# Spreading the reciprocal denominators of linear attention over 128 features: one-hot matmuls into PSUM, or a DMA inside SBUF that repeats each row 16 times

## The chip, the cores and the metric

The kernel runs on one core of one Trainium2 chip. The metric is the device time of one execution in microseconds (us), as the median of several runs. Engines are named as in the profile: PE is the matmul engine and PEld its weight load, DVE the vector engine, ACT the scalar engine, POOL the general one, SP the engine whose queue issues the DMAs. Each engine works through its own list of instructions in order and waits on semaphores for the others.

## The reference: what is computed

The input x has 2048 tokens of 512 features. Four layers follow each other, attention A, dense B, A, B, each added to its input. An A layer has 32 heads of 16 features:

```
q, k, v = split_heads(layernorm(x) @ wqkv)
pq, pk  = phi(q), phi(k)                    # phi(t) = t+1 for t > 0, else exp(t); + 1e-6
kv  = sum over tokens of pk^T v             # 16 x 16 a head
z   = sum over tokens of pk                 # 16 a head
o   = (pq @ kv) / (pq . z + 1e-6)           # one denominator for each token and head
x   = x + merge_heads(o) @ wo
```

A B layer is `x + relu(layernorm(x) @ w1) @ w2` with 1376 hidden features.

The change concerns the division. A denominator belongs to a head, and it has to reach the 16 features of that head.

## The kernel before, in words

**Tiling.** Tokens go in four chunks t of 512. The feature-by-token tiles of phi(q) stand in the SBUF tensor `big`, one unit of 128 features x 512 tokens (bf16) for each chunk t and feature group j = 0..3, so a unit holds 8 heads. All matmuls but the transposes and the warm-up are issued by one helper, `mm_group`, so they all show as line 507 and are told apart by their tiles.

**An A layer** runs in this order (`layer_steps`, L739 to L817). `p1(t)`: k projections and phi (L490, L492, L494, L500), and the sums z. `pq(t)`: q projections of chunks 0 to 2. `bar` (L763): the last sums z and the masked table `Zc` (L541); the denominators `a_den(t)` of chunks 0 to 2; the products `a_g` of xn with phi(k) for four row blocks m; `a_g_evac` (GT, L556 or L557); `a_kv`; `a_m`, which masks kv into `KVT` (L566) and multiplies it with wo into `Mf` (L573 or L574); then the q projections and the denominator of chunk 3. `p2(t)` (L784): `a_fin` for four token tiles, which multiplies phi(q) with `Mf` and adds the residual (L518); layernorm for the next layer (L436 to L461), and its transposition into `Tb`, for chunk 0 on PE (L478), for the others by a DMA on SP (L464).

**The denominators.** `a_den(t)` multiplies phi(q) with `Zc`, which puts the eight heads of group j on rows 32j to 32j+7 of one PSUM bank. ACT takes the logarithm (`lnd`, L592) and the exponential of its negative (`rdc`, L594), so `rdc` holds reciprocals in bf16. `a_pqs(t)` (L597) then multiplies each reciprocal into the 16 features of its head: four matmuls with the one-hot table `Esel` (32 rows x 128 columns each) spread the rows into four PSUM banks, and DVE multiplies `big` by each of them (L603). `Esel` is made once at the start by `head_rows` (L417), with one transposition (L419) and one DVE copy (L421).

**What sets the order.** The program is a graph of operations, each with an engine, the keys that it reads and writes, and an assumed cost in ns. `_list_schedule` (L117) walks it once on the host: of the operations that are ready within a window of each engine's list it takes the one that starts first, and so fixes for each engine a static order. It also gives out the eight PSUM banks. `a_pqs` takes four banks at once. A DMA is an operation of the SP queue with an assumed 60 ns of issue; its data are assumed to land 1.4 us after the issue at the earliest, plus the transfer time that its caller gives, one after the other over all DMAs, plus 0.6 us (L225 to L229). The multiply L603 is planned at 600 ns, ACT passes from PSUM at 495 ns. At run time each instruction of an engine waits for its semaphores, and everything behind it on that engine waits too.

Of the kernel before, what the change touches and what calls it, by code (L numbers as in the profile page):

```python
# [7 lines left out]
ALU = alu_op_type.AluOpType  # L8
ACTF = mybir.ActivationFunctionType
BF16 = mybir.dt.bfloat16  # L10
F32 = mybir.dt.float32

PE, ACT, DVE, POOL, SP = "pe", "act", "dve", "pool", "sp"
# [3 lines left out]
C_MM128 = 58.0  # L17
# [8 lines left out]
C_DVE_PSUM = 600.0  # L26
# [217 lines left out]
def build_kernel(nc, A_x, A_wqkv, A_wo, B_w1, B_w2, out, n_layers_pairs=2, K_STT=0, Q_STT=0, A_PE_CHUNKS=1, windows=None,  # L244
# [10 lines left out]
    NCH = NT // 4  # L255
# [9 lines left out]
    with es:  # L265
        def sb(name, shape, dt):
            return es.enter_context(nc.sbuf_tensor(name, list(shape), dt))
# [10 lines left out]
        KVT = sb("KVT", [128, 4, 128], BF16)  # L278
        Mf = sb("Mf", [128, 4, 512], BF16)
        NL = 2  # L280
        lnd = sb("lnd", [128, NL, 512], F32)
        rdc = sb("rdc", [128, NCH, 512], BF16)
        hm128 = sb("hm128", [128, 4, 32], BF16)
        hm1 = sb("hm1", [128, 4, 32], F32)
        Esel = sb("Esel", [128, 128], BF16)
        Zc = sb("Zc", [128, 4, 32], BF16)
        ones1 = sb("ones1", [128, 2], BF16)
        lnw = sb("lnw", [128, 2], F32)
        big = sb("big", [128, UNITS * 512], BF16)
# [21 lines left out]
        ident = sb("ident", [128, 128], BF16)  # L311
        bmask = sb("bmask", [128, 128], BF16)
        ps = es.enter_context(nc.psum_tensor("ps", [128, 8, 512], F32))
# [4 lines left out]
        g = _Graph()  # L318
# [4 lines left out]
        def alloc_bank():  # L323
            return g.new_tile()
# [7 lines left out]
        psv = _PS()  # L332
# [3 lines left out]
        def dma(emit, reads, writes, xfer_ns, name):  # L336
            sem = es.enter_context(nc.semaphore("dsem%d" % len(dma_sems)))
            dma_sems.append(sem)

            def _emit(eng, emit=emit, sem=sem):  # L340
                return emit(eng).then_inc(sem, 16)
            op = g.add(SP, _emit, reads, writes, dur=C_SP_ISSUE, lat=xfer_ns, dma=True, name=name)
            op.seq = sem
            return op
# [14 lines left out]
        def unit_ap(u, p=128):  # L359
            return big[0:p, u * 512:(u + 1) * 512]  # L360
# [30 lines left out]
        if WARM > 0:  # L391
            wt = alloc_bank()

            def _warm(e):
# [18 lines left out]
              [("onesf",)], [("hm1",)], 350, name="as_h1")  # L413
        g.add(POOL, lambda e: e.affine_select(hm128[:], hm1[:], [[0, 4], [16, 32]], ALU.is_ge, 0.0, base=15, channel_multiplier=-1),
              [("hm1",)], [("hm128",)], 350, name="as_h2")

        def head_rows():  # L417
            b = alloc_bank()
            g.add(PE, lambda e: e.transpose(psv[:, b, 0:64].bitcast(BF16), hm128[:].rearrange("p j r -> p (j r)"), ident[:]),  # L419
                  [("hm128",), ("ident",)], [("ps", b)], C_MM128, name="trh")  # L420
            g.add(DVE, lambda e: e.tensor_copy(Esel[:], psv[:, b, 0:64].bitcast(BF16)), [("ps", b)], [("Esel",)], 200.0, name="esel")  # L421

        def ln_stats_first(i):
            g.add(DVE, lambda e: e.bn_stats(bst[:, i, :], xin[:, i, :]), [("xin", i)], [("bst", i)], C_DVE_BNST, name="bnst%d" % i)  # L424
# [78 lines left out]
        def mm_group(mk, reads, writes, dur, name):  # L503
            def _emit(e, mk=mk):
                last = None
                for (o, l, r, st, sp, skip) in mk():
                    last = e.matmul(o, l, r, start=st, stop=sp, skip_group_check=skip)  # L507
                return last
            return g.add(PE, _emit, reads, writes, dur, name=name)
# [45 lines left out]
        def a_g_evac(m, GB):  # L555
            g.add_flex([(ACT, lambda e: e.activation(GT[:, m, :], psv[:, GB, :], ACTF.Identity), C_ACT_PSUM),  # L556
                        (DVE, lambda e: e.tensor_copy(GT[:, m, :], psv[:, GB, :]), C_DVE_FLEX)],  # L557
                       [("ps", GB)], [("GT", m)], name="gev%d" % m)
# [27 lines left out]
        def a_den(t):  # L586
            b = alloc_bank()
            s = scr_state["ln"]
            scr_state["ln"] = (s + 1) % NL
            mm_group(lambda: [(psv[32 * j:32 * j + 32, b, :], Zc[:, j, :], unit_ap(pq_unit(j, t)), True, True, False) for j in range(4)],  # L590
                     [("Zc",)] + [("big", pq_unit(j, t)) for j in range(4)], [("ps", b)], 400.0, "den%d" % t)
            g.add(ACT, lambda e: e.activation(lnd[:, s, :], psv[:, b, :], ACTF.Ln, bias=1e-6, scale=1.0),  # L592
                  [("ps", b)], [("lnd", s)], C_ACT_PSUM, name="lnd%d" % t)
            g.add(ACT, lambda e: e.activation(rdc[:, t, :], lnd[:, s, :], ACTF.Exp, scale=-1.0),  # L594
                  [("lnd", s)], [("rdc", t)], C_ACT_EXP, name="rdc%d" % t)

        def a_pqs(t):  # L597
            bs = [alloc_bank() for _ in range(4)]
            mm_group(lambda: [(psv[:, bs[j], :], Esel[32 * j:32 * j + 32, :], rdc[32 * j:32 * j + 32, t, :], True, True, False) for j in range(4)],
                     [("Esel",), ("rdc", t)], [("ps", b) for b in bs], 400.0, "rdx%d" % t)  # L600
            for j in range(4):
                u = pq_unit(j, t)
                g.add(DVE, lambda e, j=j, u=u: e.tensor_tensor(unit_ap(u), unit_ap(u), psv[:, bs[j], :], ALU.mult),  # L603
                      [("ps", bs[j]), ("big", u)], [("big", u)], C_DVE_PSUM, name="pqs%d_%d" % (t, j))

        def a_fin(i, first_layer):
            t, il = i // 4, i % 4
# [117 lines left out]
            tr_state["first"] = False  # L725
            transpose_chunk(t, extra_reads=extra)
        ln_first(0)
        head_rows()

        def ln_next(t, on_pe=False):  # L730
            ln_chunk(t, False)
# [7 lines left out]
        def layer_steps(layer):  # L739
            first_layer = layer == 0  # L740
            last_layer = layer == NLAYERS - 1
            steps = []
            if layer % 2 == 0:
                ZB = alloc_bank()
                KB = alloc_bank()
                GB = [alloc_bank() for _ in range(4)]

                def p1(t):
                    if first_layer and t + 1 < NCH:
                        ln_first(t + 1)  # L750
                    for i in range(4 * t, 4 * t + 4):
                        a_k(i)
                    if t >= 1:
                        for i in range(4 * t - 4, 4 * t):
                            a_z(i, ZB)
                    if first_layer and t >= 1:
                        for m in range(2):
                            a_g(m, 4 * t - 4, GB[m])

                def pq(t):  # L760
                    a_q(t)

                def bar():  # L763
                    for i in range(NT - 4, NT):
                        a_z(i, ZB)
                    a_zc(ZB)
                    for t in range(NCH - 1):
                        a_den(t)
                    n = 0
                    for m in range(4):  # L770
                        for s in range(NCH - 1 if (first_layer and m < 2) else 0, NCH):
                            a_g(m, 4 * s, GB[m])
                            n += 1
                            if n in (3, 5, 7):
                                a_pqs((n - 3) // 2)
                        a_g_evac(m, GB[m])
                        if m >= 1:
                            a_kv(m - 1, KB)
                    a_kv(3, KB)
                    a_m(KB)  # L780
                    a_q(NCH - 1)
                    a_den(NCH - 1)

                def p2(t):  # L784
                    for i in range(4 * t, 4 * t + 4):
                        a_fin(i, first_layer)
                    ln_next(t, t < A_PE_CHUNKS)
                    if t == 0:
                        a_pqs(NCH - 1)

                if first_layer:
                    for t in range(NCH):
                        steps.append((t, None, lambda t=t: p1(t)))
                        if t < NCH - 1:
                            steps.append((None, None, lambda t=t: pq(t)))
                else:
                    for t in range(NCH):
                        steps.append((t, None, lambda t=t: p1(t)))
                    for t in range(NCH - 1):
                        steps.append((None, None, lambda t=t: pq(t)))  # L800
                steps.append((None, None, bar))
                for t in range(NCH):
                    steps.append((None, t, lambda t=t: p2(t)))
            else:
                def o_step(t):
                    for i in range(4 * t, 4 * t + 4):
                        b_out(i, last_layer)
                    if last_layer:
                        store_chunk(t)
                    else:  # L810
                        ln_next(t)
                for t in range(NCH):
                    steps.append((t, None, lambda t=t: b_h(t)))
                    if t >= 1:
                        steps.append((None, None if last_layer else t - 1, lambda t=t: o_step(t - 1)))
                steps.append((None, None if last_layer else NCH - 1, lambda: o_step(NCH - 1)))
            return steps  # L817
# [129 lines left out]
```

## Time and profile before

| What | Value |
|---|---|
| Median of three runs | 295.43 us (295.38 to 295.44) |
| Profiled execution | 295.29 us, of which the span of the instructions is 293.6 us |
| PE busy | 286.7 us, 98% |
| ACT busy | 172.3 us, 59% |
| DVE busy | 156.8 us, 53% |
| POOL busy | 33.0 us, 11% |
| Granted PE clock, all 40 slices | nine tenths or more |
| DMA traffic | 15.66 MB; queue q1 busy 21.5% of 16 engines |

The table is read from the top: the profiled execution is 0.14 us under the median, and 1.69 us of it lie outside the span. A busy PE is not PE at its peak, since matmuls are pipelined: a 128x512 matmul shows as some 380 ns, while in a row of sixteen the starts are 0.216 us apart. Lines are given with a start in us from the beginning of the span, a duration, engine, line, operation, the tiles out<-in, and in square brackets the idle time of that engine before it with what ended it. The first A layer reaches its `bar` at about 46 us and the next layer at about 72 us; the second A layer does so at about 178 and 212 us.

### The profile page before, as it was taken

To read this page: it belongs to the slowest core of one execution; us is meant where nothing else is said; L and a number is where in the kernel's file an instruction comes from. 1 tells how busy PE (TensorE), PEld (TensorE's weight loads), DVE (VectorE), ACT (ScalarE), POOL (GpSimd) and SP (SyncE) were. 2 spreads that over 40 slices of the span, in tenths; PEclk is the share of its full clock that TensorE was granted. 3 is DMA by queue.
4 is the path that set the end of the run, shared out by engine and by line. 5 is a ranking of instruction groups with operands and counts; after the bars stand their busy time and mean duration, and the time that the engine had idled before them with its cause. 6 is when DMAs were issued, how large, how long until landed. Compare 5 with 4: busy or idle time off the path is not lost.

```text
span 293.6 us, 4046 instructions
## 1 busy us (share of the span) xinstructions
PE 286.7 (98%) x1540; PEld 132.0 (45%) x1540; DVE 156.8 (53%) x441; ACT 172.3 (59%) x352; POOL 33.0 (11%) x43
## 2 busy tenths in 40 slices
PE   7899999999999999999999999999999999999996
PEld 3354444334444444444444443444444444444444
DVE  5899674999700481351453758938971036020123
ACT  2997596687865484388334899258786406307000
POOL 3102100002500050020020300000260002000000
PEclk9999999999999999999999999999999999999999
DMA  7993310000330034030006300000033002301022
GB/s 224 356 370 73 65 18 0 2 0 1 74 71 0 0 65 80 1 71 2 0 0 74 73 0 2 0 0 2 1 71 74 0 0 73 73 5 66 0 74 71
DMA packets 33443, 15.66 MB, mean 53 GB/s; under 512 B 25264, under 2 KB 32912, under 8 KB 33424
## 3 DMA queue, kind: packets, MB, share of 16 engines
q1 hardware_dynamic: 33424, 15.40, 21.5%
q8 instruction: 12, 0.20, 0.3%
q14 instruction: 7, 0.06, 0.1%
HBM read 7.01 MB, written 2.10 MB: 31 GB/s over the span
## 4 chain that ended last, share of the span: by engine, by line
PE 88%; DVE 6%; DMA 2%; ACT 2%; SPq 1%; issue 0%
PE ps L507 88%; DMA xin<-in_A_x_dram 2%; DVE big L603 2%; DVE xn L456 1%; DVE xres L518 1%; ACT Mf L573 1%; ACT big L490 1%; PE ps L478 0%; DVE bst L424 0%; DVE big L500 0%; DVE emscr L494 0%; ACT sqscr L524 0%; SPq L371 0%; ACT escr L492 0%; SPq L370 0%
## 5 line engine op out<-in xcount | busy, mean ns | idle before, releaser
L507 PE MATMUL ps<-w,big 128*128 128x512 bf16 (+2 forms) x363 | 77.3, 372 | 0.0
L507 PE MATMUL ps<-Tb,w 128*128 128x512 bf16 (+1 forms) x352 | 77.1, 379 | 0.0
L628 ACT ACTIVATE big<-ps 128x512 bf16<-128x512 f32 (+1 forms) x73 | 43.2, 599 | 27.9 <-PE ps L507 27.7
L524 ACT ACTIVATE sqscr<-xres 128x512 bf16<-128x512 f32 x48 | 30.0, 629 | 41.5 <-DVE xres L518 40.6
L507 PEld LDWEIGHTS ps<-Tb,w 128*128 128x128 bf16 (+1 forms) x352 | 35.2, 100 | 40.9
L507 PEld LDWEIGHTS ps<-w,big 128*128 128x128 bf16 (+1 forms) x363 | 35.2, 97 | 40.3
L490 ACT ACTIVATE big<-ps 128x512 bf16<-128x512 f32 x64 | 41.0, 644 | 8.0 <-PE ps L507 7.8
L518 DVE SCALAR_TENSOR_TENSOR xres<-ps,xres 128x512 f32<-128x512 f32 x32 | 21.9, 687 | 41.3 <-PE ps L507 41.1
L492 ACT ACTIVATE escr<-ps 128x512 bf16<-128x512 f32 x64 | 41.3, 662 | 0.4 <-DVE emscr L494 0.4
L444 POOL TENSOR_TENSOR rstd<-veps,nhalf 128x4 f32<-128x4 f32 x15 | 16.1, 1072 | 203.8 <-DVE veps L442 183.6
L515 DVE TENSOR_TENSOR xin<-ps,xres 128x512 bf16<-128x512 f32 x15 | 10.4, 692 | 48.3 <-PE ps L507 48.3
L507 PE MATMUL ps<-wqkv,Tb 128*128 128x512 bf16 x128 | 29.6, 379 | 1.4 <-ACT Tb L482 1.1
L507 PE MATMUL ps<-Tb,wqkv 128*128 128x512 bf16 x128 | 30.6, 379 | 0.0
L507 PE MATMUL ps<-Mf,big 128*128 128x512 bf16 x128 | 29.5, 379 | 1.0 <-ACT Mf L573 0.8
L507 PE MATMUL ps<-big,xn 128*128 128x512 bf16 x128 | 30.3, 379 | 0.0
L494 DVE TENSOR_SCALAR emscr<-escr 128x512 bf16<-128x512 bf16 x64 | 18.3, 294 | 18.7 <-ACT escr L492 18.6
L500 DVE TENSOR_TENSOR big<-big,emscr 128x512 bf16<-128x512 bf16 x64 | 26.3, 420 | 1.2
L603 DVE TENSOR_TENSOR big<-big,ps 128x512 bf16<-128x512 bf16 x32 | 19.8, 678 | 1.3 <-PE ps L507 1.3
L507 PEld LDWEIGHTS ps<-wqkv,Tb 128*128 128x128 bf16 x128 | 12.1, 98 | 16.2 <-ACT Tb L482 1.5
L507 PEld LDWEIGHTS ps<-Mf,big 128*128 128x128 bf16 x128 | 11.9, 98 | 16.2 <-ACT Mf L573 1.3
L507 PEld LDWEIGHTS ps<-big,xn 128*128 128x128 bf16 x128 | 11.5, 97 | 13.1 <-issue 1.5
L507 PEld LDWEIGHTS ps<-Tb,wqkv 128*128 128x128 bf16 x128 | 11.5, 97 | 12.3 <-DVE big L603 0.4
(69 smaller groups left out, 181.2 us busy)
## 6 DMA issues: line engine op xcount, KB each, us to landing
wqkv<-in_A_wqkv_dram SPq DMA_DIRECT2D x3, 512.0 KB, 6.1
xin<-in_A_x_dram SPq DMA_DIRECT2D x3, 512.0 KB, 7.9
out_dram<-xin SPq DMA_DIRECT2D x3, 512.0 KB, 2.9
w<-in_B_w_dram SPq DMA_DIRECT2D x1, 1376.0 KB, 10.9
w<-in_B_w_dram SPq DMA_DIRECT2D x1, 1280.0 KB, 12.9
wo<-in_A_wo_dram SPq DMA_DIRECT2D x1, 512.0 KB, 8.9
xin<-in_A_x_dram SPq DMA_DIRECT2D x1, 384.0 KB, 3.0
out_dram<-xin SPq DMA_DIRECT2D x1, 256.0 KB, 2.1
```

Of the source, the lines that this page charges most:

```text
L444: g.add(POOL, lambda e: e.tensor_tensor(rstd[:, sl], veps[:, sl], nhalf[:, 0:4], ALU.pow), [("veps", t), ("nhalf",)], [("rstd", t)], C_POO ...
L456: (DVE, lambda e: e.tensor_scalar(xn[:, i, :], src, rstd[:, i:i + 1], nbias[:, i:i + 1], ALU.mult, ALU.add), C_DVE_NORM_BF if first else 4 ...
L490: g.add(ACT, lambda e: e.activation(dst_ap, psv[:, b, :], ACTF.Identity, bias=1.0 + 1e-6, scale=1.0), [("ps", b)], [dst_key], C_ACT_PSUM, ...
L492: g.add(ACT, lambda e: e.activation(escr[:, s, :], psv[:, b, :], ACTF.Exp), [("ps", b)], [("escr", s)], C_ACT_EXP, name=name + "_exp")
L494: g.add(DVE, lambda e: e.tensor_scalar(emscr[:, s, :], escr[:, s, :], 1.0, 1e-6, ALU.min, ALU.add), [("escr", s)], [("emscr", s)], C_DVE_B ...
L500: g.add(DVE, lambda e: e.tensor_tensor(dst_ap, dst_ap, emscr[:, s, :], ALU.max), [dst_key, ("emscr", s)], [dst_key], 340.0, name=name + "_ ...
L507: last = e.matmul(o, l, r, start=st, stop=sp, skip_group_check=skip)
L515: g.add(DVE, lambda e: e.tensor_tensor(xin[:, i, :], psv[:, b, :], src, ALU.add), [("ps", b), skey], [("xin", i)], C_DVE_PSUM, name="resid ...
L518: g.add(DVE, lambda e: e.scalar_tensor_tensor(xres[:, i, :], psv[:, b, :], 0.0, src, ALU.add, ALU.add, accum_out=s1[:, i:i + 1]), [("ps", ...
L524: g.add(ACT, lambda e: e.activation(sqscr[:, q, :], xres[:, i, :], ACTF.Square, accum_out=s2[:, i:i + 1]), [("xres", i)], [("sqscr", q), ( ...
L603: g.add(DVE, lambda e, j=j, u=u: e.tensor_tensor(unit_ap(u), unit_ap(u), psv[:, bs[j], :], ALU.mult), [("ps", bs[j]), ("big", u)], [("big" ...
L628: g.add_flex([(ACT, lambda e, M=M, b=b, u=u: e.activation(unit_ap(u, M), psv[0:M, b, :], ACTF.Relu), C_ACT_PSUM), (DVE, lambda e, M=M, b=b ...
```

## The change

`head_rows`, `Esel` and the four one-hot matmuls of `a_pqs` go. A tensor `rdx` in SBUF, two buffers of four groups, takes the spread reciprocals. A new step `a_spread(t)` issues four DMAs on SP, one for each group j: source are the eight rows of `rdc` (8 partitions x 512 bf16), each named 16 times by a broadcast, destination the 128 partitions of `rdx`. The multiply on DVE reads `rdx` in place of PSUM, and the scheduler is told 340 ns for it. Chunks 0 and 1 are spread right after their own denominators in `bar`, chunk 2 after the multiplies of chunk 0 (it takes the same buffer), chunk 3 after its own denominator.

```
+        NRD = 2
...
-        Esel = sb("Esel", [128, 128], BF16)
+        rdx = sb("rdx", [128, NRD, 4, 512], BF16)
...
+        def a_spread(t):
+            for j in range(4):
+                dma(lambda e, j=j: e.dma_start(rdx[:, t % NRD, j, :], rdc[32 * j:32 * j + 8, t, :].unsqueeze(1).broadcast_to([8, 16, 512])),
+                    [("rdc", t)], [("rdx", t % NRD, j)], 400.0, "rdx%d_%d" % (t, j))
+
         def a_pqs(t):
-            bs = [alloc_bank() for _ in range(4)]
-            mm_group(lambda: [(psv[:, bs[j], :], Esel[32 * j:32 * j + 32, :], rdc[32 * j:32 * j + 32, t, :], True, True, False) for j in range(4)],
-                     [("Esel",), ("rdc", t)], [("ps", b) for b in bs], 400.0, "rdx%d" % t)
             for j in range(4):
                 u = pq_unit(j, t)
-                g.add(DVE, lambda e, j=j, u=u: e.tensor_tensor(unit_ap(u), unit_ap(u), psv[:, bs[j], :], ALU.mult),
-                      [("ps", bs[j]), ("big", u)], [("big", u)], C_DVE_PSUM, name="pqs%d_%d" % (t, j))
+                g.add(DVE, lambda e, j=j, u=u: e.tensor_tensor(unit_ap(u), unit_ap(u), rdx[:, t % NRD, j, :], ALU.mult),
+                      [("rdx", t % NRD, j), ("big", u)], [("big", u)], 340.0, name="pqs%d_%d" % (t, j))
...
-        head_rows()
...
                     for t in range(NCH - 1):
                         a_den(t)
+                        if t < NRD:
+                            a_spread(t)
...
                             if n in (3, 5, 7):
                                 a_pqs((n - 3) // 2)
+                                if n == 3:
+                                    a_spread(NRD)
...
                     a_den(NCH - 1)
+                    a_spread(NCH - 1)
```

More of the change, by code (lines that the diff above doesn't have):

```diff
@@ L415, in build_kernel @@
               [("hm1",)], [("hm128",)], 350, name="as_h2")
[L417 to L421, printed above, removed]
         def ln_stats_first(i):
```

## The prediction

> **What bounds the kernel now.** I read the busy table first, then the chain of work that ended last, then the groups of the lines that the change touches, then the timeline around them.
>
> ```profile
> PE 286.7 (98%) x1540; PEld 132.0 (45%) x1540; DVE 156.8 (53%) x441; ACT 172.3 (59%) x352; POOL 33.0 (11%) x43
> PE 88%; DVE 6%; DMA 2%; ACT 2%; SPq 1%; issue 0%
> L500 DVE TENSOR_TENSOR big<-big,emscr 128x512 bf16<-128x512 bf16 x64 | 26.3, 420 | 1.2
> L603 DVE TENSOR_TENSOR big<-big,ps 128x512 bf16<-128x512 bf16 x32 | 19.8, 678 | 1.3 <-PE ps L507 1.3
> ```
>
> PE is busy for 98% and makes 88% of the chain, so a PE instruction that goes is worth its own place in PE's row, and DVE time is worth nothing except where DVE stands in the chain. The third line is the form that the changed multiply takes (both inputs and output in SBUF, bf16): 420 ns. The fourth is the multiply as it is: 678 ns.
>
> The timeline of the first A layer's `bar` shows what the one-hot matmuls cost:
>
> ```profile
> 49.07 1.03 PE L507 MATMUL ps<-big,xn 128*128 128x512 bf16 x4
> ...
> 50.03 0.39 PE L507 MATMUL ps<-rdc,Esel 32*128 32x512 bf16 x4
> ...
> 50.36 0.40 PE L507 MATMUL ps<-GT,wqkv 128*128 128x128 bf16 x4
> ...
> 50.48 4.87 DVE L603 TENSOR_TENSOR big<-big,ps 128x512 bf16<-128x512 bf16 x8 [0.74 <-PE ps L507]
> ...
> 55.27 0.68 DVE L566 TENSOR_TENSOR KVT<-ps,bmask 128x512 bf16<-128x512 f32 x1
> ...
> 59.03 1.25 PE L507 MATMUL ps<-Mf,big 128*128 128x512 bf16 x5 [0.80 <-ACT Mf L573]
> ```
>
> The four one-hot matmuls run beside each other: together they show 0.39 us, one alone 0.384. Their price is not 4 x 0.384. The four matmuls before them start at 49.07 and at their pace of 0.216 us would hand over at 49.93; PE's next other work starts at 50.36. So a group costs 0.43 us. Further down, DVE works through eight multiplies without a break, `KVT` comes behind them, and `Mf` behind `KVT`: PE waits 0.80 us for it.
>
> The end of each A layer is shown by the chain in order of time:
>
> ```profile
> 65.72 0.70 DVE xres L518 x2
> 66.42 1.20 DVE big L603 x2
> 67.62 0.07 DVE nbias L446
> 67.69 0.60 DVE big L603
> 68.29 1.01 DVE xn L456 x2
> 69.30 0.59 DVE big L603
> 69.89 0.62 DVE xres L518 x2
> ```
>
> Here DVE sets the end for 4.8 us: the multiplies of chunk 3 stand among the residuals and norms. Busy time by stretch says the same: DVE 10.96 us of the 11.60 between 59.0 and 70.6. PE has other `a_fin` work until the last of it and stands for only 0.27 us, waiting for a residual to free a bank. The second A layer repeats this at 205 to 210 us (0.28 us), but not the wait for `Mf`: between 178.3 and 198.6 PE is busy for all 20.30 us.
>
> **The change part by part**, against the profiled execution's 295.29 us.
>
> *One-hot matmuls removed.* Eight groups (four chunks, two A layers) at 0.43 us: 3.4 us. I worked out each of the eight in the same way; seven give 0.43, one 0.48. They all stand in stretches where PE has no break, so I count the whole: **-3.4**.
>
> *Setting up Esel removed.* One transposition of 0.22 us and one copy of 0.23 us, at 7.0 to 7.5 us; DVE then sits idle until a load lands at 9.72, and PE waits at 7.88 for ACT's evacuation of the first transposed tile. 0 counted; without that cover it would be 0.1 us of PE's pace.
>
> *The multiply from SBUF.* 32 x (678 - 420) = 8.3 us of DVE. It pays only where DVE is in the chain: 4 x 0.26 = 1.0 us in each chunk-3 stretch, of which PE can take no more than its bank wait, 0.27 and 0.28. I count **-0.3** for both together, since the new transfer takes part of it back. Its bounds are 0 and -0.6.
>
> *The transfers.* 32 DMAs of 128 KB, 1 KB a row, four at a time. No transfer of this kind stands in the trace, so I bound it. Nearest above: the transposing DMA, the only one from SBUF to SBUF, lands after 4.3 us (512 KB). Nearest below: the 64 KB store, 1.5 us. The 128 KB load of 1 KB rows lands after 2.0 us and the 128 KB store after 1.7; size and row length are those of the new transfer, so I take 2.0. The first issues at the start of the program follow each other by 0.46 to 0.52 us, against the 0.06 us that the scheduler assumes, so four land one after the other, the last 3 x 0.48 + 2.0 = 3.4 us after the reciprocals are there; by the bounds 2.9 to 5.7. The whole of them adds 4 MB to 15.66 MB on queues that stand idle around each `bar` (DMA share 0.01 in that stretch).
>
> *The wait in chunk 3.* Reciprocals ready at 64.99 (start 64.37, 0.62 long). Last landing 68.4, last multiply 0.42 later at 68.8; before, the last multiply ended at 69.9. So there is 1.1 us in hand in the first layer; in the second (205.09, 209.72) 0.8. But the order on DVE is static: behind the first waiting multiply stand norms and residuals, which free banks for PE. DVE had two multiplies to do from 66.3 and now gets the first data at 67.0, some 0.7 us idle, against 1.0 us saved. I count **+0.2** a layer, +0.4, for work that ends up behind a wait; bounds 0 and, with 5.7 us, (64.99 + 5.7 + 0.42) - 69.9 = 1.2 and 1.6, thus 2.8.
>
> *The wait in `bar`, first layer.* Eight transfers from 49.4: the last lands at 49.4 + 7 x 0.48 + 2.0 = 54.8, its multiply ends at 55.2. `KVT` started at 55.27 behind the same multiplies, so it moves little. The multiplies of chunk 2 now wait for their own transfers, so DVE can share the evacuation of `Mf`, which ACT did alone (four in 2.06 us). PE's 0.80 us can shrink; I count **-0.2**, with 4.3 us a transfer it grows by 2.2 (49.4 + 3.4 + 4.3 + 0.4 = 57.5 against 55.27), with 1.5 us the whole 0.8 goes. In the second layer `KVT` waits for PE at 195.5, 12 us after the reciprocals: nothing.
>
> *Queues.* SP has no other issue between 33.5 and 76.2 us, nor between 164.6 and 216.3, so the new issues pass nothing and hold nothing up, unless the planner puts one that waits ahead of a transposition; the first of those after each `bar` comes over 7 us later. The spread of chunk 2 waits for the multiplies of chunk 0, and only that of chunk 3 is behind it on SP. POOL and ACT get nothing new. Four banks fewer are held at each spread; no wait for a bank stands in either `bar` beyond those named.
>
> Sum: -3.4 - 0.3 - 0.2 + 0.4 = -3.5, thus 291.8 for the profiled execution, and 0.14 more for a median: **291.9 us**.
>
> [...]
>
> **The rivals.**
>
> *As reckoned, waits covered.* 291.9; with no stall left in `bar` and no friction 290.5, with 1.3 us more of friction 293.2. For it: 3.4 us of PE time are in the row beyond doubt. Chance 0.55.
>
> *Transfers late in the first `bar` only.* Each landing is 0.2 us further from the last than SP's pace, `KVT` comes some 1.5 us later, PE waits for `Mf`: 291.9 + 1.5 = 293.4. For it: `KVT` has 0.1 us in hand. Chance 0.17.
>
> *Slower: the waiting multiply holds DVE up.* If a transfer lands only after the 4.3 us of the transposing DMA, DVE stands with `KVT` behind it once and with residuals and norms behind it twice: 2.2 + 1.2 + 1.6 = 5.0 in place of the -0.2 and +0.4 counted. 295.29 - 3.4 - 0.3 + 5.0 + 0.1 = 296.7. It decides from the landing at which these three waits exceed 3.7 us: about 0.4 us less a transfer, 3.9. Against it: the store and load of the same size at 1.7 and 2.0. Chance 0.18.
>
> *No gain.* The matmuls go, but the time isn't PE's to give: ACT's phi passes (L490, L492) or a newly ordered plan, with 340 ns for the multiply and late landings, set the next wait. 295.3. Against it: PE's 20.30 of 20.30 us around four of the groups. Chance 0.10.
>
> **How the numbers follow.** A measurement of this kernel tells about 0.2% from no change, 0.6 us. Faster: the first two cases, 0.72. Same: 0.10. Slower: 0.18. The range leaves out most of the slow case beyond 296.0 and a little below 290.3.
>
> **What would show it.** Right: no matmul with `Esel` in the timeline, L603's successor at 420 ns, the four DMAs landing about 2 us after issue and 0.5 us apart, PE's pace unbroken where the groups stood, the multiplies of chunk 3 over before 69 us. Wrong: DVE idle before that multiply with a DMA as releaser and PE idle behind `Mf` or a residual right after it (the slow case), or PE idle before other work in `bar` without a DMA in the chain (no gain). A landing over 4 us, or an issue on SP much longer than 0.5 us, would break the forecast.

## The result and the profile after

The kernel became slower: 351.19 us (350.96 to 352.65, four runs) against 295.44 us (295.38 to 295.83) for the kernel before in the same runs, a ratio of 1.190 (95% interval 1.187 to 1.193). The prediction was 291.9 us, range 290.3 to 296.0. The profiled execution took 352.65 us, with a span of 350.9 us against 293.6: 57.3 us more.

Four lines of the page of the changed kernel answer to those shown of before: the busy times, the granted PE clock in 40 slices, the chain that ended last, and the multiply.

```profile
PE 293.0 (83%) x1483; PEld 134.2 (38%) x1507; DVE 151.2 (43%) x439; ACT 173.6 (49%) x352; POOL 34.1 (10%) x44
PEclk9999999567969999999999999965896999999999
PE 70%; DMA 18%; DVE 4%; ACT 3%; SPq 3%; issue 1%
L600 DVE TENSOR_TENSOR big<-big,rdx 128x512 bf16<-128x512 bf16 x32 | 13.6, 426 | 58.7 <-DMA rdx<-rdc 58.7
```

The multiply takes 426 ns, as forecast (420). But DVE stood idle for 58.7 us in front of it, all of it for the transfers, and PE went from 98% to 83%. The clock line, which was full throughout before, now has two dips. The chain in order of time shows where the transfers stand in it:

```profile
59.04 19.75 DMA rdx<-rdc x3
...
90.90 8.41 DMA rdx<-rdc
...
221.70 19.34 DMA rdx<-rdc x3
...
256.90 8.44 DMA rdx<-rdc
```

That is twice in each A layer, once for chunks 0 to 2 and once for chunk 3, 55.9 us in all. The timeline of the first `bar` shows the single landings as the starts of the multiplies, and who stands behind them:

```profile
55.19 0.43 DVE L600 TENSOR_TENSOR big<-big,rdx 128x512 bf16<-128x512 bf16 x1 [4.35 <-DMA rdx<-rdc]
...
57.72 0.42 DVE L600 TENSOR_TENSOR big<-big,rdx 128x512 bf16<-128x512 bf16 x1 [2.10 <-DMA rdx<-rdc]
...
60.34 0.43 DVE L600 TENSOR_TENSOR big<-big,rdx 128x512 bf16<-128x512 bf16 x1 [2.20 <-DMA rdx<-rdc]
62.64 0.43 DVE L600 TENSOR_TENSOR big<-big,rdx 128x512 bf16<-128x512 bf16 x1 [1.87 <-DMA rdx<-rdc]
65.01 0.43 DVE L600 TENSOR_TENSOR big<-big,rdx 128x512 bf16<-128x512 bf16 x1 [1.94 <-DMA rdx<-rdc]
65.35 0.68 DVE L561 TENSOR_TENSOR KVT<-ps,bmask 128x512 bf16<-128x512 f32 x1
...
66.49 1.49 PE L502 MATMUL ps<-wo,KVT 128*128 128x512 bf16 x3 [10.30 <-DVE KVT L561]
...
79.15 0.68 DVE L569 CAST Mf<-ps 128x512 bf16<-128x512 f32 x1
...
79.98 5.42 PE L502 MATMUL ps<-Mf,big 128*128 128x512 bf16 x16 [10.29 <-DVE Mf L569]
```

The first transfer was issued at 50.54 and landed after 4.6 us; the next ones followed 2.3 to 2.6 us apart. The masking of kv (L561) needs none of these data. It stands on DVE behind five multiplies, one part of `Mf` (L569) behind all twelve, and PE waits for both. In the second A layer the masking itself stands behind all twelve:

```profile
241.07 0.43 DVE L600 TENSOR_TENSOR big<-big,rdx 128x512 bf16<-128x512 bf16 x1 [1.01 <-DMA rdx<-rdc]
241.41 0.68 DVE L561 TENSOR_TENSOR KVT<-ps,bmask 128x512 bf16<-128x512 f32 x1
...
242.15 1.03 PE L502 MATMUL ps<-wo,KVT 128*128 128x512 bf16 x2 [16.55 <-DVE KVT L561]
```

The views of waits sum this up; columns are the total in us, how often, and the longest:

```profile
PE ps L502 <- DVE KVT L561: 26.9, 2, 16.6
PE ps L502 <- DVE big L600: 11.8, 2, 6.1
PE ps L502 <- DVE Mf L569: 10.3, 1, 10.3
```

These are 49.0 us. After each such wait PE runs at half clock for a time: the row of the 16 matmuls above is 5.42 us long where such a row took 3.63 before:

```profile
65.94 3.63 PE L507 MATMUL ps<-Mf,big 128*128 128x512 bf16 x16
```

In the five stretches of half clock 53 of the 128x512 matmuls have the next start 0.43 in place of 0.216 us later, 10.8 us together. The first load landed 1.1 us later in this execution. 49.0 + 10.8 + 1.1 = 60.9 us of loss; the removal itself, as the floor below shows, gave 4.7 us of span back, so 56.2 are accounted for, against 57.3 measured. Some matmul records are missing, and the sum is no closer than that.

**Theories.** The packet records of the trace show two things about the transfers. Each ends in eight completion packets where a store of 128 KB has sixteen, and for 99% of the time in which their packets move, at most eight of these are under way at once; from both I take it that a transfer runs on eight engines. And a 1 KB packet takes 140 ns in the median, against 46 ns for the loads and stores; while one transfer is under way, 48 packets start per us. Theory A: the rate is set by the stretch of partitions that the source rows lie on, eight neighbours here. Theory B: eight engines and a slow SBUF-to-SBUF packet. Theory C: a row that is read 16 times is slow.

### The profile page after: what moved, and what is told of

Its sections match the earlier page's. It is cut to its first block, busy times and chain, and to the rows that moved or that the text cites. A ratio compares the mean times of both kernels' runs of the same rounds, so it can differ in the third digit from the quotient of the medians.

```text
span 350.9 us, 3992 instructions
## 1 busy us (share of the span) xinstructions
PE 293.0 (83%) x1483; PEld 134.2 (38%) x1507; DVE 151.2 (43%) x439; ACT 173.6 (49%) x352; POOL 34.1 (10%) x44
## 4 chain that ended last, share of the span: by engine, by line
PE 70%; DMA 18%; DVE 4%; ACT 3%; SPq 3%; issue 1%
PE ps L502 70%; DMA rdx<-rdc 16%; SPq L594 2%; DMA xin<-in_A_x_dram 2%; ACT sqscr L519 1%; DVE xres L513 1%; ACT big L485 1%; DVE big L495 1%; DVE big L600 0%; ACT escr L487 0%; DVE xn L451 0%; DVE emscr L489 0%; PE ps L473 0%; DVE bst L419 0%; ACT lnd L587 0%
## 5 line engine op out<-in xcount | busy, mean ns | idle before, releaser
L502 PE MATMUL ps<-Tb,w 128*128 128x512 bf16 (+1 forms) x352 | 80.2, 390 | 0.0
L502 PE MATMUL ps<-w,big 128*128 128x512 bf16 (+3 forms) x355 | 76.0, 372 | 0.4
L625 ACT ACTIVATE big<-ps 128x512 bf16<-128x512 f32 (+1 forms) x76 | 45.1, 599 | 32.4 <-PE ps L502 32.3
L502 PEld LDWEIGHTS ps<-Tb,w 128*128 128x128 bf16 (+1 forms) x352 | 36.2, 103 | 43.9 <-issue 5.2
L502 PE MATMUL ps<-Mf,big 128*128 128x512 bf16 x124 | 33.0, 414 | 22.3 <-DVE big L600 11.8
L600 DVE TENSOR_TENSOR big<-big,rdx 128x512 bf16<-128x512 bf16 x32 | 13.6, 426 | 58.7 <-DMA rdx<-rdc 58.7
L502 PE MATMUL ps<-Tb,wqkv 128*128 128x512 bf16 x128 | 33.0, 402 | 0.0
L502 PE MATMUL ps<-wqkv,Tb 128*128 128x512 bf16 x122 | 28.6, 379 | 2.7 <-ACT Tb L477 1.2
L502 PE MATMUL ps<-big,xn 128*128 128x512 bf16 x124 | 29.5, 379 | 0.3
L502 PE MATMUL ps<-wo,KVT 128*128 128x512 bf16 x6 | 3.2, 628 | 27.1 <-DVE KVT L561 26.9
L502 PEld LDWEIGHTS ps<-wqkv,Tb 128*128 128x128 bf16 x128 | 12.1, 97 | 17.1 <-DVE Tb L478 1.7
```

Of the source, the lines that this page charges most:

```text
L625: g.add_flex([(ACT, lambda e, M=M, b=b, u=u: e.activation(unit_ap(u, M), psv[0:M, b, :], ACTF.Relu), C_ACT_PSUM), (DVE, lambda e, M=M, b=b ...
```

## The experiments

The kernel before is measured again beside each group of runs: its median was 295.72, 295.82 and 295.81 us.

### Other source partitions

First, the same eight rows and 16 repeats on partitions four apart. To have them there, each head's denominator is computed on four neighbouring rows (by the mask `hm128`):

```
- affine_select(hm1[:], ones_v, [[0, 4], [-16, 32]], ...)      # and the second mask alike
+ affine_select(hm1 as "p j (h c)", ones_v as "p j (h c)", [[0, 4], [-16, 8], [0, 4]], ...)
- rdc[32 * j:32 * j + 8, t, :].unsqueeze(1).broadcast_to([8, 16, 512])
+ rdc[32 * j:32 * j + 32:4, t, :].unsqueeze(1).broadcast_to([8, 16, 512])
```

> Each head's denominator is computed on four neighbouring rows, and the transfer reads every fourth row: eight source rows, each repeated 16 times, eight engines, as in the changed kernel, but the rows lie on partitions 32j, 32j+4, ... 32j+28 in place of 32j to 32j+7. Theory A (the source partitions set the rate: in the changed kernel eight neighbouring partitions give 48 packets of 1 KB a us together): packets go from 140 to under 80 ns, four transfers land under 1 us apart, the kernel comes to 292 to 296 us. Theory B (eight engines at 140 ns for a packet that goes from SBUF to SBUF): nothing changes, 2.5 us apart, 351 us. Theory C (a row that is read 16 times is what is slow): nothing changes, 351 us. [...]

298.03 us, ratio 1.008 (1.005 to 1.011); 53 of the 56 us are gone. Packets take 46 ns in the median, 164 to 188 start per us, a transfer still ends in eight completion packets and lands 2.5 to 3.6 us after its issue. DVE's idle time in front of the multiply falls from 58.7 us:

```profile
L600 DVE TENSOR_TENSOR big<-big,rdx 128x512 bf16<-128x512 bf16 x32 | 13.3, 422 | 12.0 <-DMA rdx<-rdc 11.6
```

Rows, repeats, engines, bytes and destination are those of the changed kernel, so B and C fall: where the rows lie is what made the transfers slow. What is left may be the eight engines: eight packets in 46 ns are 174 a us, an estimate from the two numbers.

With the same mask, all 32 rows are read, four times each (`rdc[32 * j:32 * j + 32, t, :]`, `[32, 4, 512]`):

> The same table as in the run with every fourth row, but all 32 rows of a group are read, each repeated 4 times. Theory A: the source lies on the same stretch of 32 partitions as in the run with every fourth row, transfers under 1 us apart, 292 to 296 us, and no slower than that run. Theory B (engines): if the number of engines doubles with the rows and a packet stays at 140 ns, a transfer takes 1.2 us in place of 2.5; by proportion about half of the 56 us lost, some 320 us. Theory C (repeats): 4 in place of 16 repeats a row, a quarter of the time, 0.6 us a transfer, 292 to 296 us as A.

297.08 us, ratio 1.004 (1.001 to 1.006). Sixteen completion packets, so by the same reading sixteen engines; some 180 to 210 packets a us, landings at 2.5 to 2.9 us for nearly all. Little better than eight rows on the same partitions: the number of engines is a small matter. The nine executions go from 295.12 to 298.39 us, and the granted clock of each divides them: three with 1.000 took up to 296.31, six with 0.994 took 296.63 and more.

Sixteen neighbouring rows, eight repeats:

> Each head's denominator on two neighbouring rows, 16 source rows on partitions 32j to 32j+15, each repeated 8 times. Between the changed kernel (partitions 32j to 32j+7: 48 packets a us, landings 2.5 us apart) and the run with 32 rows (landings paced by SP at 0.65 us). Theory A (the stretch of source partitions sets the rate, in proportion): about 96 packets a us, landings 1.3 us apart, PE's waits about a third to a half of the changed kernel's, 302 to 325 us. Rival (all that counted was eight against sixteen engines, or the number of repeats falling under some bound): landings 0.65 us apart as with 32 rows, 297 us.

307.04 us, ratio 1.038 (1.036 to 1.040). In the first two us, with one transfer under way, 98 and 92 packets start per us, twice the 48 of eight neighbours; where transfers of different groups overlap, up to some 180. Eight rows four partitions apart (164 to 188) beat sixteen neighbours (some 96) and, with the same eight completion packets a transfer, eight neighbours (48): neither the number of rows nor that of engines sets the rate here, the stretch of partitions does. In bytes, 48 and some 96 packets of 1 KB a us are 49 and 98 GB/s.

The changed kernel's own trace shows more of it, since the next transfer is issued before the last one lands. Group j reads from partition 32j. In the microsecond that ends 0.4 us before a landing, 45 to 52 packets start where rows 0 to 7 are followed by 32 to 39, or 64 to 71 by 96 to 103 (16 cases), but 57 to 111 where 32 to 39 are followed by 64 to 71, or 96 to 103 by 0 to 7 (12 cases). So in these transfers rows of one half (0 to 7 and 32 to 39, or 64 to 71 and 96 to 103) had together no more than one transfer alone, 48, and rows of both halves had more.

### The floor, and its parts

> The changed kernel without its 32 transfers: rdx is filled once with ones on POOL, before the first multiply, so the spreading of the reciprocals is left out; everything else stays. It is the floor of the change. If the terms of the prediction that concern PE and DVE hold (-3.4 for the matmuls, -0.3, -0.2 and no wait), 291.4 us. Rival (the time is not PE's to give): 294.8 to 296.

294.21 us, ratio 0.994 (0.992 to 0.996), and no verdict on the floor: the fill was ready to run at once and went ahead of the first layernorm on POOL (7.9 us busy in the first 20 against 4.6), PE did 15.1 us of work in those 20 in place of 17.2 and lost its clock there for 3.4 us (0.91 granted over the 20, before 1.00). The next run has no fill: the spreading is left out, the multiply reads `rdc` itself, and the four-row mask stands in it.

```
- g.add(DVE, lambda e, j=j, u=u: e.tensor_tensor(unit_ap(u), unit_ap(u), rdx[:, t % NRD, j, :], ALU.mult),
-       [("rdx", t % NRD, j), ("big", u)], ...
+ g.add(DVE, lambda e, j=j, u=u: e.tensor_tensor(unit_ap(u), unit_ap(u), rdc[:, t, :], ALU.mult),
+       [("rdc", t), ("big", u)], ...
```

> No transfers and no tensor rdx: the multiply on DVE reads the unspread reciprocals in SBUF, a tile of the same shape and type, so the spreading is left out. The floor of the change, with no fill at the start that could stand in the way of the first layernorm. If the prediction's terms for PE and DVE hold (-3.4, -0.3, -0.2): 291.2 to 292. Rival (the freed PE time is taken by other waits): 293.5 to 295.

290.73 us, ratio 0.983 (0.982 to 0.984). The change without its transfers is worth 5.1 us, more than the 3.9 that the prediction counted. With the matmuls put back in front of the multiply:

> The run that reads the unspread reciprocals, with the eight groups of one-hot matmuls put back in their place, and the multiply waiting for them as in the kernel before; only the operand of the multiply stays in SBUF (the spread values are not used). It splits the floor of 290.7 into the part of PE and the part of DVE. By the prediction's terms: matmuls 3.4, so 290.7 + 3.4 = 294.1; the multiply alone is worth about 1 us. Rival (the faster multiply is worth more than counted, since DVE stands in front of KVT and Mf): 292.5 to 293.5.

294.43 us, ratio 0.996 (0.995 to 0.997). So the matmuls are 294.43 - 290.73 = 3.7 us (counted 3.4), the faster multiply 295.81 - 294.43 = 1.4 us (counted 0.5 with the wait for `Mf`).

### The traffic without its readers

> The kernel before, with its one-hot matmuls, and the 32 transfers of the changed kernel beside them into a tensor that nobody reads. If the loss is all in the waits of the multiplies for the transfers, the time stays within 0.3% of before, 294.8 to 296. If the traffic itself slows the engines (access to SBUF) or holds up the transposing DMAs behind it on SP, it rises by several us; each transposition that is held up would show it as a wait of PE for Tb.

304.68 us, ratio 1.030 (1.027 to 1.032). Nobody reads the data, and 9 us are lost all the same. The first line is SP's issue of the next transpositions in the kernel before; the others are the same issue in this kernel and PE's matmul that needs the first transposition:

```profile
76.25 5.72 SPq L464 DMA_TRANSPOSE Tb<-xn  x2
...
81.21 7.33 SPq L466 DMA_TRANSPOSE Tb<-xn  x2
...
89.00 3.59 PE L509 MATMUL ps<-Tb,w 128*128 128x512 bf16 x8 [6.56 <-DMA Tb<-xn]
```

The transposition is issued 5.0 us later, because the last of the spreading transfers is still being issued until 81.1: SP spends up to 2.63 us on one of them. And it lands 7.8 us after its issue in place of 4.7, behind their last packets, which start until 86.4. PE's wait of 6.6 us follows, and then half clock: the next weight loads start 0.43 us apart.

> The kernel before with its matmuls, and the 32 transfers in the form with 32 rows repeated 4 times beside them, read by nobody (Esel scaled by a quarter). With the eight-row transfers beside it the kernel before went from 295.7 to 304.7, and PE waited 6.6 us for a transposition that stood behind them on SP. If that was their slowness alone, now within 0.5 us of before, 295.3 to 296.3. If traffic or issues in themselves cost, 298 and more.

295.61 us, ratio 1.000 (0.999 to 1.001); the transposition is issued at 76.63 and lands 4.6 us later. 32 more issues and 4 MB more cost nothing measurable as long as the transfers are fast.

### The order that the scheduler makes

One number in the changed kernel, source rows as they were:

```
-                    [("rdc", t)], [("rdx", t % NRD, j)], 400.0, "rdx%d_%d" % (t, j))
+                    [("rdc", t)], [("rdx", t % NRD, j)], 2500.0, "rdx%d_%d" % (t, j))
```

> The changed kernel with one number changed: the scheduler is told 2500 ns in place of 400 for each spreading transfer, about what they took, and orders the engines anew. The masking of kv then stands ahead of the multiplies. Theory P (most of the loss comes from the order that the wrong 400 ns made, work queued behind waiting multiplies): the waits of 10, 10 and 17 us before KVT and Mf go, 300 to 310 us. Theory L (the transfers themselves are too late: 16 a layer at 2.5 us are 40 us, and PE has some 25 us of work from the first denominator to the last a_fin): 12 to 15 us a layer stay, 320 to 330 us.

310.01 us, ratio 1.048 (1.047 to 1.050): 41 of the 56 us are gone with transfers as slow as before. The longest waits of PE in this kernel:

```profile
PE ps L502 <- DVE big L600: 4.4, 2, 3.2
PE ps L473 <- DVE xn L451: 4.0, 1, 4.0
PE ps L502 <- DVE big L495: 3.5, 2, 3.1
```

No `KVT` and no `Mf` among them. Theory P holds for the larger part. 14 us stay for the transfers being late, half of what theory L gave them.

Then both mended, 32 rows and true costs (the last number is the time that an issue occupies SP, 60 ns before; with 500 ns of transfer the scheduler expects a landing 2.5 us after the issue):

```
- dma(lambda e, j=j: e.dma_start(rdx[:, t % NRD, j, :], rdc[32 * j:32 * j + 8, t, :].unsqueeze(1).broadcast_to([8, 16, 512])),
-     [("rdc", t)], [("rdx", t % NRD, j)], 400.0, "rdx%d_%d" % (t, j))
+ dma(lambda e, j=j: e.dma_start(rdx[:, t % NRD, j, :], rdc[32 * j:32 * j + 32, t, :].unsqueeze(1).broadcast_to([32, 4, 512])),
+     [("rdc", t)], [("rdx", t % NRD, j)], 500.0, "rdx%d_%d" % (t, j), 650.0)
```

> 32 source rows repeated 4 times, and the scheduler is told what such a transfer takes: 650 ns of issue on SP in place of 60, landing 2.5 us after the issue. If what is left of the loss with 32 rows (297 against 295.7 us) is KVT and Mf behind multiplies that wait in the first bar, and the half clock after it, both go: 291.5 to 293.5 us, near the floor without transfers. Rival (the landing itself, 2.6 us after the reciprocals, and SP's 0.65 us an issue are what costs): 296 to 298.

293.85 us (293.76 to 294.26), ratio 0.994 (0.993 to 0.995): faster than the kernel before by 0.6%. Against the run with 32 rows and the wrong costs, the end of the first `bar` there was

```profile
59.86 0.43 DVE L600 TENSOR_TENSOR big<-big,rdx 128x512 bf16<-128x512 bf16 x1 [0.19 <-DMA rdx<-rdc]
60.21 0.68 DVE L569 CAST Mf<-ps 128x512 bf16<-128x512 f32 x1
...
61.04 3.57 PE L502 MATMUL ps<-Mf,big 128*128 128x512 bf16 x10 [2.82 <-DVE Mf L569]
```

with `Mf` behind the twelfth multiply, and ten matmuls in 3.57 us after the wait, which is half clock for most of them; with the true costs it is

```profile
53.97 0.69 DVE L561 TENSOR_TENSOR KVT<-ps,bmask 128x512 bf16<-128x512 f32 x1
...
55.46 0.69 DVE L569 CAST Mf<-ps 128x512 bf16<-128x512 f32 x1
...
57.31 2.97 PE L502 MATMUL ps<-Mf,big 128*128 128x512 bf16 x13
```

`Mf` stands between the multiplies, and PE reaches it without a wait and at full clock. Of the 3.1 us that are left to the floor, 1.8 are two waits in chunk 3 of the first A layer, in the same kernel:

```profile
69.19 1.21 PE L473 MATMUL ps<-ident,xn 128*128 128x128 bf16 x16 [0.86 <-DVE xn L451]
...
71.32 1.04 PE L502 MATMUL ps<-Mf,big 128*128 128x512 bf16 x4 [0.92 <-DVE big L600]
```

For the rest, PE's busy time in the two profiles is 0.7 us less in the first 20 us, 0.3 in the first `bar` (46 to 59) and 0.3 at 200 to 215.

Chunk 3 by matmuls again, the others by transfers:

> The run with 32 source rows and the true costs in the plan, but chunk 3 of each A layer goes by one-hot matmuls again (Esel scaled by a quarter, since four rows hold each reciprocal); chunks 0 to 2 go by transfers. If what still separates 293.85 from the floor of 290.7 without transfers is chunk 3, whose reciprocals come late (1.0 and 1.1 us of PE's time before the transpositions and the last a_fin of the first A layer): -2.1 for these waits, +0.43 twice for the matmuls, 292.6 us. Rival (the rest is in the bar, or PE's four banks at that place cost as much): 293.5 to 295.

293.97 us, ratio 0.994 (0.993 to 0.996): no better, the rival was right. The matmuls cost their share, the multiply is back at 678 ns on a DVE that is full there, and PE still waits in front of the transpositions (0.63 us).

> Eight source rows, every fourth partition, each repeated 16 times, with the scheduler told 650 ns of issue and 740 ns a transfer. With eight engines a transfer has 16 packets of 46 ns on each, 0.74 us, against SP's 0.65 us an issue; with 32 rows it has half that. If eight engines cost only this 0.09 us a transfer: within 0.8 us of the run with 32 rows, 294 to 294.7. If the number of engines costs more in its own right: over 296.

295.19 us, ratio 0.997 (0.995 to 1.000), from 293.70 to 296.67 over twelve runs: inconclusive. The best runs equal those with 32 rows, so the eight engines need not cost anything. Four of the twelve had a granted clock of 0.993 to 0.994 and took 295.74 to 296.67, the eight with 0.999 or 1.000 took 293.70 to 295.52; why these differ among themselves stays open.

## Why the prediction was wrong

**The step that failed** is "The transfers": "I take 2.0 ... four land one after the other, the last 3 x 0.48 + 2.0 = 3.4 us after the reciprocals are there; by the bounds 2.9 to 5.7". Measured, the first lands after 4.4 to 4.6 us and the fourth some 12 us after the reciprocals. The price of a lone landing was off by 2.5 us, just past its upper bound of 4.3; the price of the spacing was taken from SP's issue pace, 0.48 us, and had no bound from the data side at all. It is 2.1 to 2.6 us. The 0.2 us more a landing in the rival with a late first `bar` was my estimate, and no run shows it. Every row that I took for "size and row length" spreads 128 rows over 128 partitions, on the SBUF side; this transfer reads eight neighbouring ones. The run with rows four apart shows that this alone made the transfers slow. Even with fast transfers SP issues one every 0.65 us and a landing takes 2.6, a third more than 0.48 and 2.0.

**A second step had no price.** The prediction saw that the scheduler assumes 0.06 us for an issue that takes some 0.5, and counted nothing for the order that follows from such numbers. With the transfers as slow as they are, the order made for 400 ns cost 41 us against the one made for 2500. With fast transfers in the old plan the change still takes 297.08 us, outside the range; it comes to 293.85, inside, only when the plan has their true costs too.

**The number of engines**, eight by the completion packets, is not what made the transfers slow: the run with eight spread rows has eight too, and packets of 46 ns; the changed kernel has packets of 140 ns.

**The rival for slower had the mechanism**, a waiting multiply with `KVT`, residuals and norms behind it, in the places named, and a price of 5.0 us where the waits made 49.0. Two parts of it were missing. "In the second layer ... nothing" was false: the static order there puts all twelve multiplies ahead of `KVT`, and PE waits for 16.6 us, the longest wait of all. A wait's place in the old order need not be its place in the new one. And the clock: PE's waits were followed by matmuls at 0.43 us, 10.8 us of loss that no term held. One slip of sum is in its price: the 1.6 us of the second layer is 1.5 by its own terms (205.09 + 5.7 + 0.42 - 209.72), which changes nothing.

**The queues** ("the new issues pass nothing and hold nothing up") held only as long as the transfers are fast: with issues of some 0.6 us the transposition moved by 0.4 us and nothing was lost. With the slow transfers issues take up to 2.64 us, the transposition behind them is issued and lands late, and without any reader this cost 9 us.

**Right:** the terms of the removal. Matmuls -3.4 (measured 3.7), the multiply at 420 ns (426), and the stretch of chunk 3 as the tightest place: with fast transfers and a true plan 1.8 of the last 3.1 us are lost there. What the faster multiply is worth was put too low: -0.5 with the wait for `Mf`, 1.4 measured.

## What to carry to other kernels

Price a transfer by the partitions that it reads from, not only by its bytes and row length: a broadcast from eight neighbouring partitions ran at 49 GB/s, where the loads at the start of the kernel reach 370, and having the source rows on 32 partitions by a replicated mask cost nothing that the run with fast traffic and no readers could show. (The destination was 128 partitions in every run, so nothing is shown of that side.) Give a chain of transfers two prices, the landing of one and the spacing of many. Where a scheduler orders engines by assumed costs, a wrong cost of a new operation can cost more than the operation: here 41 of 56 us.

## What the runs showed of the hardware

- The source partitions set the rate of these transfers inside SBUF: 48 packets of 1 KB a us from eight neighbouring partitions, 92 to 98 from sixteen, 164 to 188 from eight that lie four apart, some 180 to 210 from 32. Eight neighbours and the eight 32 partitions further on (0 to 7 and 32 to 39) did not add up in the changed kernel: 45 to 52 while one transfer follows the other.
- An issue on SP for such a transfer takes 0.54 to 0.62 us for nearly all of them when the transfers are fast, and the next follows after 0.65 (the first loads of the kernel: 0.40 to 0.51); it takes up to 2.64 us when they are slow.
- PE's clock halved around most long waits: starts 0.43 in place of 0.216 us apart. In all runs together, thirteen waits of 2.39 to 16.55 us came with a stretch of half clock, of 3.4, 6.8, 10.2 or 17.1 us, that began during the wait or within 1.0 us of its end; two waits of 2.47 and 3.08 us, both in the run with sixteen neighbouring rows, and all waits up to 1.80 us began none. Length alone does not decide it.
